# Rows of a shifted operand at other addresses: z at a step of 576 words, one word ahead of a multiple of 64 words

## The chip, the cores and the metric

The kernel runs on one core of one Trainium2 chip. The metric is the device time of one execution in microseconds (us). Runs of one kernel agree within about 0.2%.

## The reference

Two layers run one after the other on x (2048 rows of 512 numbers, float32). Each layer has two parts.

```
x = x + Re(DFT_seq(DFT_hidden(LN(x))))            # part A, matmuls with given cos/sin matrices
y = LN(x)                                         # part B takes y and returns
h = gelu(LN(y) @ w1)                              #   512 -> 512
hs = concat(h[:, 0:128] shifted by +1 row, h[:, 128:256] by -1,
            h[:, 256:384] by +2, h[:, 384:512] by -2) @ w2
x1 = y + hs
B(y) = x1 + gelu(LN(x1) @ w3) @ w4                #   512 -> 1376 -> 512
x = x + B(y)
```

## The kernel before

Every product is made of three fp32r matmuls: a number is split into a high part (its fp32r rounding, written by ACT) and a low part (the rest, written by DVE), and `mm3` (lines 277 to 280) adds high x high, high x low and low x high into one PSUM bank. The matrix that is multiplied is loaded as weights, 128 columns at a time (LDWEIGHTS), and the other operand streams past it, 512 float32 words a matmul. The two operands of a profile row are the ones it reads; for the matmuls on z the weights are w1 (`w`) and z (`zt`) streams.

Each layer first computes part A, in four chunks of 512 rows, and then calls `by_pairs`, which is part B. `by_pairs` begins with the same four chunks in order: `shifted(c)` is the product with w1 and the shift, `mixed(c)` the product with w2. After chunk 3 come two pairs of chunks of the MLP with w3 and w4, and while the second pair of layer 0 is worked on, part A of layer 1 is prepared.

**z.** The twice-normalized rows of a chunk, turned so that channels lie on the partitions, are called z: 4 channel tiles of 128, and for each a row of high parts and a row of low parts, 512 columns plus a halo of 2 columns at each end (`SW` = 516 words). There are two buffers: `zt[0]` for even chunks and `zt[1]` for odd ones (line 91); `ztf` are the same places read as plain float32. The shift of part B is done by reading: for the channel group g, `shifted` streams 512 words from the row's column 2 + `SHIFT[g]`, with `SHIFT` = (-1, 1, -2, 2), for each of the 4 channel tiles, so 12 matmuls a group. The groups run in the order -1, -2, +1, +2.

**How z is filled.** The normalized rows are turned by DVE, stored to DRAM (`turn_out`, line 600, four transfers on the SP queue) and fetched back as float32 into the places of the low parts (`turn_in`, line 605, one transfer of all four channel tiles). ACT then writes the high parts (`z_highs`, `high` at line 422) and DVE the low ones in place (`z_lows`, `low` at line 425), in two instructions each, two channel tiles at a time (`z_half`). The halo columns are zero at the ends of the sequence (`edges`), or copied from the chunk before by POOL (`left_halo`, line 626), or taken from the first two rows of the next chunk, which PE transposes (`right_halo`, lines 619 to 623). `turn_in` of chunk 1 is issued while chunk 0 is multiplied, and so on.

**Order.** The work beside the matmuls is laid into slots by hand: eight slots a chunk (four groups of `shifted`, four row tiles of `mixed`); `D(slot, ...)` runs ahead of the slot's own evacuation and `A(slot, ...)` after it. In each of them the instructions go to their engine's queue in the order written. SP issues all transfers in order, and the transfers signal their landing on eight semaphores that are used in turn.

**Places.** One arena of SBUF holds everything; tensors are placed by hand at word offsets from its start, which is byte 640 of each partition. `ZW` = 4128 words is the room of one z buffer; both stand at the arena's start. The weights w1 and w2 (`w12`, from word 8256), the streamed DFT blocks (`ring`) and the MLP's blocks all begin at multiples of 64 words. The four raw buffers (from `RAWS`, 1024 words each) receive DFT blocks and w1, w2 from DRAM in part A; in part B the same words are `rest[0]` to `rest[7]` (512 words each): `rest[0:4]` hold rows of odd chunks, `rest[4:8]` are used in the MLP pairs. Buffers that overlap are kept apart by waits that the framework puts in from the order of the program.

Of the kernel before, what the change touches and what calls it, by code (L numbers as in the profile page):

```python
# [8 lines left out]
F32 = mybir.dt.float32  # L9
F32R = mybir.dt.float32r  # L10
AF = mybir.ActivationFunctionType
ALU = mybir.AluOpType
# [7 lines left out]
CH = 512  # L20
NC = S // CH
TC = CH // P
KD = D // P
# [6 lines left out]
SHIFT = (-1, 1, -2, 2)  # L30
HALO = 2
SW = CH + 2 * HALO
RING = 4
RAW = 4
WARM = 12
# [7 lines left out]
def spectral_mlp_kernel(ctx: ExitStack, tc: tile.TileContext, x, ws, hs, w1, w2, w34, out):  # L43
    nc = tc.nc
# [23 lines left out]

    ZW = KD * 2 * SW
    AX, AY = 3 * 2 * DH, 4 * 2 * DH  # L70
# [5 lines left out]
    base = -(-nc.sbuf_base // 32) * 32  # L76
    EXT = RNG + RING * 4 * CH
    RAWS = EXT + 6 * D
# [3 lines left out]
    def at(name, word, *shape, dtype=F32R):  # L82
        return nc.alloc_sbuf_tensor_at(name, [P, *shape], dtype, offset=base + 4 * word).ap()

    def both(name, word, *shape):
        return at(name, word, *shape), at(name + "f", word, *shape, dtype=F32)
# [1 line left out]
    ay_at = (0, AY, H3, H3 + AY, EXT, 2 * AY, 3 * AY, 4 * AY)  # L88
    ay, ayf = zip(*(both(f"ay{k}", ay_at[k], 4, 2, DH) for k in range(NP)))
    ax, axf = zip(*(both(f"ax{k}", XS - 8 * D + k * AX, 3, 2, DH) for k in range(NP)))  # L90
    zt, ztf = zip(*(both(f"zt{i}", i * ZW, KD, 2, SW) for i in range(2)))
    w12 = [at(f"w12{i}", W12 + i * 4 * CH, 2, 2, CH) for i in range(4)]
    beside = at("beside", XS - 4 * D - 2 * HALO * KD * 2, 4, D, dtype=F32)
    xs = [at(f"xs{i}", XS + i * 2 * D, 2, D, dtype=F32) for i in range(NP)]
# [4 lines left out]
    rg = [[at(f"rg{i}{g}", RR + (4 * i + g) * 2 * CH, 2, CH) for g in range(KD)] for i in range(2)]  # L99
    ring, ringf = zip(*(both(f"ring{i}", RNG + i * 4 * CH, 2, 2, CH) for i in range(RING)))  # L100
    raw_at = [at(f"raw{i}", RAWS + i * 2 * CH, 2, CH, dtype=F32) for i in range(RAW)]
# [25 lines left out]
    def mm_bank():  # L127
        count["mm"] += 1
        return mm4[(count["mm"] - 1) % 4]
# [13 lines left out]
    def piece(src, a=0, b=2):  # L143
        pieces.append((src, a, b))
        return len(pieces) - 1
# [9 lines left out]
    for layer in range(LAYERS):  # L155
        for c in range(NC):
# [5 lines left out]
            for k in range(NP):  # L162
# [4 lines left out]
                p = piece(ws[c, k][:, 2:4])  # L167
# [42 lines left out]
    def stage_one():  # L210
# [4 lines left out]
        if dest is None:  # L215
            dest = ring[state["made"] % RING]
            sums[n] = ringf[state["made"] % RING][:, :, 1]
            state["made"] += 1
# [15 lines left out]
    def stage_two():  # L234
        n = state["two"]
        kind, ids, (a, b), _ = items[n]
        dest = slots[n]
        hi, lo = dest[:, a:b, 0], dest[:, a:b, 1]
        src = raws[ids[0]][:, a:b] if kind == "plain" else sums.pop(n)[:, a:b]
        for i in ((1, 0) if n == 1 else (slice(0, b - a),)):  # L240
            nc.vector.tensor_tensor(lo[:, i], src[:, i], hi[:, i].bitcast(F32), op=ALU.subtract)  # L241
        state["two"] += 1
        issue_dma()

    def room():
# [3 lines left out]
        if items[n][3] is not None:  # L249
            return True  # L250
        return state["made"] - state["done"] < RING

    def prefetch():
        n = state["one"]
        while room():
            stage_one()
            while state["two"] < state["one"] - 1:
                stage_two()
        while state["two"] < n:
            stage_two()  # L260
# [5 lines left out]
    def stream():  # L266
        i = state["use"]
        if i and items[i - 1][3] is None:
            state["done"] += 1
        state["use"] += 1  # L270
        prefetch()
        while state["two"] <= i:
            stage_two()
        return slots.pop(i)


    def mm3(o, lh, ll, rh, rl, first, last):
        nc.tensor.matmul(o, lh, rh, start=first, stop=False)  # L278
        nc.tensor.matmul(o, lh, rl, start=False, stop=False)  # L279
        nc.tensor.matmul(o, ll, rh, start=False, stop=last)  # L280
# [140 lines left out]
    def high(tf):  # L421
        nc.scalar.copy(tf[0][:, :, 0], tf[1][:, :, 1])

    def low(tf):
        nc.vector.tensor_tensor(tf[0][:, :, 1], tf[1][:, :, 1], tf[0][:, :, 0].bitcast(F32), op=ALU.subtract)
# [40 lines left out]
    def run_late(*names):  # L466
        for i in names:
            for f in late.pop(i, ()):
                f()
# [132 lines left out]
    def turn_in(dst, col):  # L602

        z = zd[count["turn"] % 2].rearrange("(d p) t -> p d t", p=P)
        nc.sync.dma_start(dst[:, :, 1, col : col + CH], z)

    def edges(c):

        if c == 0:
            nc.vector.memset(zt[0][:, :, :, :HALO].bitcast(F32), 0.0)  # L610
            left_halo(1)
        if c == NC - 1:
            nc.vector.memset(zt[c % 2][:, :, :, HALO + CH :].bitcast(F32), 0.0)

    def right_halo(c, u):

        ps = mm_bank()
        for d in range(KD):
            nc.tensor.transpose(ps[:, d * B : (d + 1) * B], u[:B, d * P : (d + 1) * P], ident[:B, :B])
        v = ps[:, : KD * B].rearrange("p (d t) -> p d t", d=KD)[:, :, :HALO]  # L620
        hi, lo = (zt[c % 2][:, :, i, HALO + CH :] for i in range(2))
        nc.scalar.copy(hi, v)
        nc.vector.tensor_tensor(lo, v, hi.bitcast(F32), op=ALU.subtract)

    def left_halo(c):
        nc.gpsimd.tensor_copy(zt[c % 2][:, :, :, :HALO], zt[(c - 1) % 2][:, :, :, CH : CH + HALO].bitcast(F32))

    def gelu(g, ps):
        order = "p (q b j) -> p b q j", "p (b q j) -> p b q j"
# [17 lines left out]
    def gelu_split(dst, ps, copy=nc.vector.tensor_copy):  # L647
        g = tmp_tile()
        gelu(g, ps)
        split(dst, g, copy)  # L650

    def shifted(c, w1p, hook=None, copy=nc.vector.tensor_copy, pre=None):

        for n, g in enumerate((0, 2, 1, 3)):
            ps = mm_bank()
            w = slice(HALO + SHIFT[g], HALO + SHIFT[g] + CH)
            for d in range(KD):
                s = w1p[d // 2][:, d % 2]
                z = zt[c % 2][:, d]
                v = slice(g * P, (g + 1) * P)  # L660
                mm3(ps, s[:, 0, v], s[:, 1, v], z[:, 0, w], z[:, 1, w], d == 0, d == KD - 1)
            if pre:
                pre(n)
            gelu_split(rg[c % 2][g], ps, copy)
            if hook:
                hook(n)
# [54 lines left out]
    def last_of(layer):  # L721
        return layer == LAYERS - 1

    def z_half(c, i):
        return [t[c % 2][:, 2 * i : 2 * i + 2, :, HALO : HALO + CH] for t in (zt, ztf)]

    def by_pairs(layer, zs, xin, dst):
        act = nc.scalar.copy
# [4 lines left out]
        turn_out(turned01)  # L733
        state["limit"] += 2
        w2p = [stream(), stream()]
        us = [[tmp[:, i] for i in range(4)], rest[0:4]]
        x1s, mrs, todo = {c: us[c % 2] for c in range(NC)}, {c: [] for c in range(NC)}, {}

# [49 lines left out]
            return lambda: [low((blk[b], blkf[b])) for b in names]  # L788

        def z_highs(c):  # L790
            return lambda: [high(z_half(c, i)) for i in range(2)]

        def z_lows(c):
            return lambda: [low(z_half(c, i)) for i in range(2)]

# [233 lines left out]
        for pair in range(n_pairs):  # L1031
# [11 lines left out]
            if pair == 0:  # L1043
                t = tmp[:, 0:4]
# [18 lines left out]
            for i, names in enumerate((("11", "21"), ("12", "22"))):  # L1063
                for d in range(KD):
                    b = blk[names[d // 2]]
                    v = slice(d * P, (d + 1) * P)
# [33 lines left out]
            for p in range(NF // 2):  # L1100
                prep = {} if kept else w_prep(p)
                u, v, x, y = sets[p % 2]
                w = w3b[(5 * pair + p) % 2]
# [89 lines left out]
            if last:  # L1193
                ss = [w4_use(), w4_use()]
                for q in range(TC):
                    v = slice(q * P, (q + 1) * P)
# [3 lines left out]
                    j = c2 * TC + q  # L1200
# [9 lines left out]
    for layer in range(LAYERS):  # L1210
# [4 lines left out]
        for c in range(NC):  # L1215
            if layer == 0 and c == 0:
# [58 lines left out]
                def hook(i):  # L1275
                    k, odd = divmod(i, 2)
                    state["limit"] = w_items[layer]
                    if not odd:
                        if k + 1 < NP:
                            xp_norm(k + 1, 3)  # L1280
                            xp_main(k + 1)
                        if not k:
                            xp_main_lows(1)
                    else:
                        if 0 < k < NP - 1:
                            xp_main_lows(k + 1)
                        if k + 2 < NP:
                            xp_stats(k + 2)
                        if k:
                            xp_sums(k - 1)  # L1290
                            xp_highs(k - 1, False)
                            xp_lows(k - 1, False)
# [62 lines left out]
        for i, (ri, dp) in enumerate(HORDER):  # L1355
            if i == 1:
                run_late("im1")
            if i == 3:
                state["limit"] += 2
            s = stream()  # L1360
            hid(ri, dp, s, acc4, 0, i == 0, i == 3)
            if i == 0:
                turn_in(ztf[0], HALO)
            if i < 2:
                j = (6, 8)[i]
                rows(xs[j // 2], x1d, j, 2, True)
            if i == 0:
                run_late("re1", "im1+")
            if i == 1:
                for half in range(2):  # L1370
                    high(z_half(0, half))
                run_late("re0+", "re0++")
                zs.update(norm_z((4, 5)))
            if i == 2:
                run_late("re0")
                for half in range(2):
                    low(z_half(0, half))
                zs.update(norm_z((6, 7)))
        by_pairs(layer, zs, xin, out if last_layer else x2d)

# [52 lines left out]
```

## Time and profile before

| what | value |
|---|---|
| median of 3 runs | 1445.81 us (1445.06 to 1447.05) |
| the profiled execution | 1445.1 us, span 1443.0 us, granted TensorE clock 1.000 |
| PE busy | 1434.9 us, 99% of the span, 6312 matmuls |
| DVE, ACT, POOL busy | 1127.5, 714.2, 82.2 us |
| DMA | 291.06 MB, mean 202 GB/s |
| chunks of `shifted` and `mixed`, layer 0 | about 410 to 500 us of the span |
| the same, layer 1 | about 1123 to 1213 us |

A row of instructions grouped by line reads: line, engine, operation, out<-in by the program's names, shape, count | busy us, mean ns of one | idle time of the engine before them and what ended it. A row in order of time reads: start us, length us, engine, line, operation, out<-in, and in brackets the idle time before it. The lengths of matmuls are longer than the distance between their starts, since they overlap. The chain of waits follows the work that ended last back from the end, at each step to what released it.

### The profile page before, as it was taken

The page shows a single profiled execution, that of the slowest core. Times are in us where ns is not written, and L with a number is a line of the kernel's source. Part 1 is how long each engine was busy: PE and PEld are TensorE (multiplying, and loading weights), DVE is VectorE, ACT ScalarE, POOL GpSimd, SP SyncE. Part 2 cuts the span into 40 slices and gives each one's busy share as a digit, 9 for nine tenths or more (in the row PEclk, how much of TensorE's full clock was granted, in tenths as well). Part 3 has the DMA queues.
Part 4 walks back from the last instruction along what each step waited for, and adds up shares of the span by engine and source line. Part 5 has one row for each costly group of instructions (what it writes and reads, how often), then busy time and mean ns, then how long its engine had stood idle before and what let it go on. Part 6 is the DMA issues. An engine that isn't in the chain of part 4 may idle for free.

```text
span 1443.0 us, 17233 instructions
## 1 busy us (share of the span) xinstructions
PE 1434.9 (99%) x6312; PEld 1180.7 (82%) x6312; DVE 1127.5 (78%) x1559; ACT 714.2 (49%) x954; POOL 82.2 (6%) x111
## 2 busy tenths in 40 slices
PE   9999999999999999999999999999999999999998
PEld 7888888888888787888888888888888888888887
DVE  7876997987979889656799979879898787656443
ACT  5563454455566755434555544544455574433231
POOL 2100000000001000000000000000000010000000
PEclk9999999999999999999999999999999999999999
DMA  7326655657655758954645556465766466579434
GB/s 251 128 88 206 202 188 198 198 181 258 205 173 136 265 206 289 363 196 164 216 158 195 175 197 211 161 227 167 228 224 233 132 175 262 182 244 338 155 130 161
DMA packets 116068, 291.06 MB, mean 202 GB/s; under 512 B 8592, under 2 KB 41360, under 8 KB 113424
## 3 DMA queue, kind: packets, MB, share of 16 engines
q1 hardware_dynamic: 115984, 289.97, 59.7%
q8 instruction: 49, 0.80, 0.2%
q14 instruction: 35, 0.29, 0.1%
HBM read 243.01 MB, written 46.92 MB: 201 GB/s over the span
## 4 chain that ended last, share of the span: by engine, by line
PE 88%; DVE 6%; ACT 2%; DMA 2%; issue 1%; SPq 0%; POOL 0%; DVEq 0%; ACTq 0%; POOLq 0%
PE psd L278 9%; PE psd L280 9%; PE psd L279 9%; PE psa L278 7%; PE psa L280 7%; PE psa L279 7%; PE psc L278 6%; PE psc L279 6%; PE psc L280 6%; PE psb L278 6%; PE psb L279 6%; PE psb L280 6%; DMA w4r<-w4d 1%; DVE st L292 1%; DMA zt1f<-zd 1%
## 5 line engine op out<-in xcount | busy, mean ns | idle before, releaser
L223 ACT CAST ring<-raw 128x1024 fp32r<-128x1024 f32 x127 | 133.1, 1053 | 99.8 <-PE psd L280 51.1
L241 DVE TENSOR_TENSOR ring<-raw,ring 128x1024 fp32r<-128x1024 f32 (+1 forms) x128 | 154.6, 1212 | 25.0 <-ACT ring L223 25.0
L278 PE MATMUL psd<-ring,rr 128*128 128x512 f32 x208 | 80.9, 389 | 0.0
L279 PE MATMUL psd<-ring,rr 128*128 128x512 f32 x208 | 80.9, 389 | 0.0
L280 PE MATMUL psd<-ring,rr 128*128 128x512 f32 x208 | 80.9, 389 | 0.0
L631 ACT ACTIVATE tmp<-rest 128x512 f32<-128x512 f32 x36 | 22.7, 632 | 94.8 <-DVE rest L464 94.5
L318 POOL TENSOR_TENSOR rs<-ve,mhalf 128x4 f32<-128x4 f32 x16 | 27.8, 1738 | 610.9 <-DVE nm L317 610.9
L230 ACT CAST ring<-ring0f 128x1024 fp32r<-128x1024 f32 x28 | 29.6, 1056 | 58.2 <-DVE ring0f L229 58.2
L634 DVE TENSOR_TENSOR h<-hc,h 128x512 fp32r<-128x512 f32 x41 | 27.9, 689 | 36.3 <-ACT h L637 34.6
L241 DVE TENSOR_TENSOR ring<-ring1f,ring 128x512 fp32r<-128x512 f32 (+1 forms) x56 | 53.3, 951 | 0.7 <-ACT ring L226 0.7
L297 POOL TENSOR_TENSOR rs<-ve,mhalf 128x2 f32<-128x2 f32 (+1 forms) x33 | 28.1, 853 | 417.2 <-DVE nb L296 417.2
L637 ACT CAST h<-hc 128x512 fp32r<-128x512 f32 x41 | 25.4, 621 | 51.2 <-PE psd L279 17.0
L279 PE MATMUL psb<-ring,ay 128*128 128x512 f32 x128 | 50.0, 391 | 0.0
L279 PE MATMUL psc<-ring,ay 128*128 128x512 f32 x128 | 49.9, 390 | 0.0
L280 PE MATMUL psb<-ring,ay 128*128 128x512 f32 x128 | 49.8, 389 | 0.0
L278 PE MATMUL psc<-ring,ay 128*128 128x512 f32 x128 | 49.8, 389 | 0.0
L280 PE MATMUL psc<-ring,ay 128*128 128x512 f32 x128 | 49.8, 389 | 0.0
L278 PE MATMUL psb<-ring,ay 128*128 128x512 f32 x128 | 49.8, 389 | 0.0
L280 PE MATMUL psa<-ring,ay 128*128 128x512 f32 x126 | 49.0, 389 | 0.0
L279 PE MATMUL psa<-ring,ay 128*128 128x512 f32 x126 | 49.0, 389 | 0.0
L278 PE MATMUL psd<-ring,ay 128*128 128x512 f32 x126 | 49.0, 389 | 0.0
L279 PE MATMUL psd<-ring,ay 128*128 128x512 f32 x126 | 49.0, 389 | 0.0
(444 smaller groups left out, 4417.3 us busy)
## 6 DMA issues: line engine op xcount, KB each, us to landing
raw<-in_ws SPq DMA_DIRECT2D x183, 512.0 KB, 4.9
w4r<-w4d SPq DMA_DIRECT2D x77, 512.0 KB, 4.1
raw<-in_hs SPq DMA_DIRECT2D x56, 512.0 KB, 3.6
w3b<-w3d SPq DMA_DIRECT2D x15, 1792.0 KB, 7.5
w3d<-w3b SPq DMA_DIRECT2D x5, 1792.0 KB, 6.3
x1d<-tmp SPq DMA_DIRECT2D x12, 512.0 KB, 6.2
xs<-x1d SPq DMA_DIRECT2D x12, 512.0 KB, 6.4
w4d<-w4r SPq DMA_DIRECT2D x11, 512.0 KB, 7.6
```

The source lines that it names most:

```text
L223: nc.scalar.copy(dest[:, a:b, 0], r[0][:, a:b])
L230: nc.scalar.copy(dest[:, :, 0], lo)
L241: nc.vector.tensor_tensor(lo[:, i], src[:, i], hi[:, i].bitcast(F32), op=ALU.subtract)
L278: nc.tensor.matmul(o, lh, rh, start=first, stop=False)
L279: nc.tensor.matmul(o, lh, rl, start=False, stop=False)
L280: nc.tensor.matmul(o, ll, rh, start=False, stop=last)
L292: nc.vector.bn_stats(st[:, i], s)
L297: nc.gpsimd.tensor_tensor(rs[:, :n], ve[:, :n], mhalf[:, 0, :n], op=ALU.pow)
L318: nc.gpsimd.tensor_tensor(rs, ve, mhalf[:, :, :2], op=ALU.pow)
L631: nc.scalar.activation(g_of, ps_of, AF.Gelu_apprx_tanh)
L634: nc.vector.tensor_tensor(dst[:, 1], g, dst[:, 0].bitcast(F32), op=ALU.subtract)
L637: copy(dst[:, 0], g)
```

## The change

Rows of z lie `ZP` = 576 words apart instead of 516. Each tensor of z begins 7 words ahead of its first row, so that the rows begin at word 63, 639, ... of the arena: one word ahead of a multiple of 64 words (256 bytes), counted from the arena's start. Four tiles of 2 x 576 words and a second such buffer don't fit in the room, so the odd chunks' buffer has three channel tiles there, and the fourth in the words of raw buffers 2 and 3 (`rest[4]` to `rest[6]`), which nothing else uses while z of an odd chunk lives. Each z is now a list of tensors (one for even chunks, two for odd), and everything that touches z goes through them: `turn_in`, `right_halo` and `left_halo` take one instruction for each tensor, `z_parts` gives pieces of two, one and one channel tiles for odd chunks. `left_halo(1)` moves from `edges(0)` to after the staging of w2 (in `by_pairs`, behind `w2p = [stream(), stream()]`).

```
+ZP = 9 * 64
...
-    zt, ztf = zip(*(both(f"zt{i}", i * ZW, KD, 2, SW) for i in range(2)))
+    zt, ztf = [], []
+    for i, places in enumerate((((56, 4),), ((56 + 8 * ZP, 3), (RAWS + 4 * CH + 56, 1)))):
+        ts = [both(f"zt{i}{j}", word, 7 + n * 2 * ZP) for j, (word, n) in enumerate(places)]
+        for z, k in ((zt, 0), (ztf, 1)):
+            z.append([t[k][:, 7:].rearrange("p (d r w) -> p d r w", r=2, w=ZP)[:, :, :, :SW] for t in ts])
...
     def turn_in(dst, col):
         z = zd[count["turn"] % 2].rearrange("(d p) t -> p d t", p=P)
-        nc.sync.dma_start(dst[:, :, 1, col : col + CH], z)
+        for d, t in z_rows(dst):
+            nc.sync.dma_start(t[:, :, 1, col : col + CH], z[:, d])
+
+    def z_rows(ts):
+        at = 0
+        for t in ts:
+            yield slice(at, at + t.shape[1]), t
+            at += t.shape[1]
+
+    def z_of(c, d):
+        return next(t[:, d - v.start] for v, t in z_rows(zt[c % 2]) if v.start <= d < v.stop)
 
     def edges(c):
         if c == 0:
-            nc.vector.memset(zt[0][:, :, :, :HALO].bitcast(F32), 0.0)
-            left_halo(1)
+            for t in zt[0]:
+                nc.vector.memset(t[:, :, :, :HALO].bitcast(F32), 0.0)
...
-        hi, lo = (zt[c % 2][:, :, i, HALO + CH :] for i in range(2))
-        nc.scalar.copy(hi, v)
-        nc.vector.tensor_tensor(lo, v, hi.bitcast(F32), op=ALU.subtract)
+        for d, t in z_rows(zt[c % 2]):
+            hi, lo = (t[:, :, i, HALO + CH :] for i in range(2))
+            nc.scalar.copy(hi, v[:, d])
+            nc.vector.tensor_tensor(lo, v[:, d], hi.bitcast(F32), op=ALU.subtract)
 
     def left_halo(c):
-        nc.gpsimd.tensor_copy(zt[c % 2][:, :, :, :HALO], zt[(c - 1) % 2][:, :, :, CH : CH + HALO].bitcast(F32))
+        for d, odd in z_rows(zt[1]):
+            even = zt[0][0][:, d]
+            to, of = (even, odd) if c % 2 == 0 else (odd, even)
+            nc.gpsimd.tensor_copy(to[:, :, :, :HALO], of[:, :, :, CH : CH + HALO].bitcast(F32))
...
-                z = zt[c % 2][:, d]
+                z = z_of(c, d)
...
-    def z_half(c, i):
-        return [t[c % 2][:, 2 * i : 2 * i + 2, :, HALO : HALO + CH] for t in (zt, ztf)]
+    def z_parts(c):
+        for t, tf in zip(zt[c % 2], ztf[c % 2]):
+            for d in range(0, t.shape[1], 2):
+                yield [z[:, d : min(d + 2, t.shape[1]), :, HALO : HALO + CH] for z in (t, tf)]
...
         w2p = [stream(), stream()]
+        left_halo(1)
```

More of the change, by code (lines that the diff above doesn't have):

```diff
@@ L604, in turn_in @@
         z = zd[count["turn"] % 2].rearrange("(d p) t -> p d t", p=P)
-        nc.sync.dma_start(dst[:, :, 1, col : col + CH], z)
+        for d, t in z_rows(dst):
[7 more added lines that the diff above has]
+        return next(t[:, d - v.start] for v, t in z_rows(zt[c % 2]) if v.start <= d < v.stop)
     def edges(c):
         if c == 0:
-            nc.vector.memset(zt[0][:, :, :, :HALO].bitcast(F32), 0.0)
-            left_halo(1)
+            for t in zt[0]:
+                nc.vector.memset(t[:, :, :, :HALO].bitcast(F32), 0.0)
         if c == NC - 1:
-            nc.vector.memset(zt[c % 2][:, :, :, HALO + CH :].bitcast(F32), 0.0)
+            for t in zt[c % 2]:
+                nc.vector.memset(t[:, :, :, HALO + CH :].bitcast(F32), 0.0)
     def right_halo(c, u):
@@ L790, in z_highs @@
         def z_highs(c):
-            return lambda: [high(z_half(c, i)) for i in range(2)]
+            return lambda: [high(z) for z in z_parts(c)]
         def z_lows(c):
-            return lambda: [low(z_half(c, i)) for i in range(2)]
+            return lambda: [low(z) for z in z_parts(c)]
         fs = [NF - 1] + list(range(NF - 1))
@@ L1369, in spectral_mlp_kernel @@
             if i == 1:
-                for half in range(2):
-                    high(z_half(0, half))
+                for z in z_parts(0):
+                    high(z)
                 run_late("re0+", "re0++")
@@ L1375, in spectral_mlp_kernel @@
                 run_late("re0")
-                for half in range(2):
-                    low(z_half(0, half))
+                for z in z_parts(0):
+                    low(z)
                 zs.update(norm_z((6, 7)))
```

## The prediction

> **What bounds the kernel now.** I read the page's shares first, then the PE instructions grouped by line with shapes apart, then single PE rows in order of time, and last the chain of waits where it leaves PE.
>
> ```profile
> span 1443.0 us, 17233 instructions
> PE 1434.9 (99%) x6312; PEld 1180.7 (82%) x6312; DVE 1127.5 (78%) x1559; ACT 714.2 (49%) x954; POOL 82.2 (6%) x111
> ...
> PE 88%; DVE 6%; ACT 2%; DMA 2%; issue 1%; SPq 0%; POOL 0%; DVEq 0%; ACTq 0%; POOLq 0%
> ```
>
> PE is never free for long, and 88% of the chain is matmuls. So the time is the number of matmuls by the distance between their starts, plus a few short stalls. The change removes no matmul; it can only alter that distance, or a stall.
>
> ```profile
> L278 PE MATMUL psd<-ring,rr 128*128 128x512 f32 x208 | 80.9, 389 | 0.0
> ...
> L278 PE MATMUL psd<-zt,w 128*128 128x512 f32 x68 | 27.0, 398 | 0.0
> ...
> L278 PE MATMUL psa<-zt,w 128*128 128x512 f32 x60 | 24.1, 402 | 0.0
> ```
>
> Of matmuls of one shape, those that stream z (zt) are the long ones: 398 and 402 ns against 389. There are 384 of them: 2 layers x 4 chunks x 4 shifts x 4 channel tiles x 3 products. The durations overlap, so I price by starts. First and last rows of groups of 12 z matmuls (one chunk, one shift), and of 36 that stream w2:
>
> ```profile
> 410.28 0.40 PE L278 MATMUL psd<-zt,w 128*128 128x512 f32 x1
> ...
> 412.88 0.40 PE L280 MATMUL psd<-zt,w 128*128 128x512 f32 x1
> ...
> 416.46 0.39 PE L278 MATMUL psa<-zt,w 128*128 128x512 f32 x1
> ...
> 418.98 0.40 PE L280 MATMUL psa<-zt,w 128*128 128x512 f32 x1
> 419.21 0.40 PE L278 MATMUL psd<-zt,w 128*128 128x512 f32 x1
> ...
> 421.75 0.39 PE L280 MATMUL psd<-zt,w 128*128 128x512 f32 x1
> ...
> 424.75 0.39 PE L278 MATMUL psa<-w,rg 128*128 128x512 f32 x1
> ...
> 432.69 0.39 PE L280 MATMUL psd<-w,rg 128*128 128x512 f32 x1
> ...
> 441.85 0.40 PE L278 MATMUL psd<-zt,w 128*128 128x512 f32 x1
> ...
> 444.42 0.39 PE L280 MATMUL psd<-zt,w 128*128 128x512 f32 x1
> ...
> 481.00 0.39 PE L278 MATMUL psd<-zt,w 128*128 128x512 f32 x1
> ...
> 483.54 0.40 PE L280 MATMUL psd<-zt,w 128*128 128x512 f32 x1
> ```
>
> The ordinary distance is (432.69-424.75)/35 = 226.9 ns. Now the addresses, in words from the start of the arena. Before, rows of z begin at multiples of 516 and 4128, all multiples of 4, and a matmul starts 2 + shift words further on: one word past a multiple of 4 for shift -1, three past it for +1, on it for -2 and +2. Shift -1 (chunk 0): 2.60/11 = 236.4 ns. Shift +1: 2.52/11 = 229.1. Shift +2: 230.9 in chunk 0 and 2.57/11 = 233.6 in chunk 1. Shift -2 (chunk 3): 230.9. For starts on a multiple of 4 I use 232.0. The order of the four does not follow the order of time, so it goes with the address. The whole excess is 96 x (9.5 + 2.2 + 5.1 + 5.1) ns = 2.1 us, 0.15% of the span: the most that placement by itself can bring.
>
> **The change part by part.**
>
> (a) New starts. Rows lie 63 words past a multiple of 64, so the starts are 0 (shift -1), 2 (+1), 63 (-2) and 3 (+2) past it. Shift -1 now starts on a multiple of 64, as every ring, weight and block operand does (their offsets, 8256, 16448 and so on, are multiples of 64): between 226.9 and 232.0; I take 226.9, as the address is of the ordinary kind. Gain 96 x 9.5 = 0.91 us. Shifts -2 and +2 are now three past a multiple of 4, the class of the 229.1 row: 192 x 2.9 = 0.56 us. Shift +1 is two past it, a class that no row shows: between 226.9 and 236.4, and as it lies between the one-past and three-past classes I take the middle, 231.7, a loss of 96 x 2.6 = 0.25 us. Sum 1.22 us: 0.61 a layer, 0.31 for two chunks. Bounds: 2.1 us; and with shift -1 at 232.0, +1 at 236.4 and the others unchanged, 0.42 - 0.70 = a loss of 0.3 us.
>
> [...]
>
> (b) Smaller pieces for the odd chunks. A high or low of z was two instructions of 1024 elements; for odd chunks it is one of 1024 and two of 512.
>
> ```profile
> L637 ACT CAST h<-hc 128x512 fp32r<-128x512 f32 x41 | 25.4, 621 | 51.2 <-PE psd L279 17.0
> ...
> L634 DVE TENSOR_TENSOR h<-hc,h 128x512 fp32r<-128x512 f32 x41 | 27.9, 689 | 36.3 <-ACT h L637 34.6
> ```
>
> ```profile
> L422 ACT CAST zt<-zt1f x8: 1038/1055/1058, 424.8 to 1185.7; 128x1024 fp32r<-128x1024 f32 x8
> L425 DVE TENSOR_TENSOR zt<-zt1f,zt x8: 1226/1227/1228, 427.0 to 1188.1; 128x1024 fp32r<-128x1024 f32 x8
> L626 POOL CAST zt<-zt x6: 198/200/1229, 407.3 to 1165.5; 128x16 fp32r<-128x16 f32 x6
> ...
> L622 ACT CAST zt<-psa x3: 158/158/158, 437.1 to 1172.9; 128x8 fp32r<-128x8 f32 x3
> ```
>
> ACT: 2 x 621 - 1055 = 0.19 us more four times; DVE: 2 x 689 - 1227 = 0.15 us more four times. The right halo of chunk 1 has one more ACT piece of 0.16 us and one more DVE piece; each left halo one more POOL piece of 0.20 us. POOL is busy 6%, ACT 49%: I price these at nothing except where (d) shows DVE to be late; without that cover they would add about 0.5 us a layer.
>
> (c) The left halo of chunk 1 moves behind both transposes and the staging of w2, because its last tile's place is raw buffer 2 and 3, which w2's lows still read.
>
> ```profile
> 407.26 1.21 POOL L626 CAST zt<-zt 128x16 fp32r<-128x16 f32 x1 [45.18 <-ACT w L223]
> ...
> 411.89 2.31 DVE L241 TENSOR_TENSOR w<-raw,w 128x1024 fp32r<-128x1024 f32 x2
> ...
> 418.73 0.38 SPq L605 DMA_DIRECT2D zt1f<-zd  x1
> ```
>
> It can run from 414.20 instead of 407.26, 1.2 us or less a piece. Nothing else stands behind it on POOL then. SP's transfer, which fills the same buffers, issues at 418.73, and the first matmul that reads the halo follows the row at 432.69. It passes the four stores of turned z on SP, which do not touch it. Cost nothing, with 2 us to spare.
>
> (d) The transfer of z in two, for odd chunks: three tiles, then one; same bytes, one issue (0.38 us) more. This matters in one place, layer 0, chunk 3, where the chain leaves PE at the end of chunk 1 and comes back 46 us later:
>
> ```profile
> 444.85 0.61 ACT extra L631
> ...
> 490.57 0.61 DVE rg L634
> 491.18 0.04 issue
> 491.23 0.50 PE psa L280
> ```
>
> ```profile
> 463.81 0.89 SPq L605 DMA_DIRECT2D zt1f<-zd  x1
> ...
> 470.73 0.80 ACT L326 ACTIVATE tmp<-xs,nb,rs 128x512 f32<-128x512 f32 x1
> 472.36 2.14 ACT L422 CAST zt<-zt1f 128x1024 fp32r<-128x1024 f32 x2 [0.84 <-DMA zt1f<-zd]
> ...
> 474.59 2.49 DVE L425 TENSOR_TENSOR zt<-zt1f,zt 128x1024 fp32r<-128x1024 f32 x2 [2.45 <-ACT zt L422]
> ...
> 490.23 0.39 PE L279 MATMUL psa<-w,rg 128*128 128x512 f32 x1
> 491.23 0.50 PE L280 MATMUL psa<-w,rg 128*128 128x512 f32 x1 [0.61 <-DVE rg L634]
> ```
>
> PE loses 1.00 - 0.23 = 0.77 us there. The first low of z waited for both highs (it starts 0.09 us after 472.36 + 2.14), although it reads only the first's tiles. With the last tile a buffer of its own, it should wait for the first two pieces only: 472.36 + 1.06 + 0.62 + 0.11 = 474.15, and lows of 1.23 + 0.69 + 0.69 end at 476.8 against 477.08: 0.3 us earlier. The first transfer, three quarters of the bytes, can also land earlier; ACT has been free since 471.53, so that is worth 0 to 0.83 us; it shares the queue with stores, and I take a quarter, 0.2. Relief 0.5 us (bounds -0.2, if DVE waits for all three highs, and 1.1).
>
> **The sum.** In layer 0 the chain goes with PE to 444.85 (0.31 us gained by two chunks), then with DMA, ACT and DVE (0.5 us). PE itself arrives 0.61 us earlier at 490, so 0.57 us of stall remain and what is gained is 0.8 us, not 0.61 + 0.77. Layer 1 shows no such stall and keeps its 0.61 us. Total 1.4 us. The profiled execution took 1445.1 us (span 1443.0), 0.7 below the median of the runs, 1445.81; taken from the median, 1444.4 us.
>
> **The rivals.** 1, all of it: shift +1 and the others also come down to 226.9 and the stall goes: 2.1 + 0.8 = 2.9 us, 1442.9. For it: every other operand runs at 226.9. Against: no start three past a multiple of 4 does so in the groups shown.
>
> [...]
>
> 3, slower: the transfers go round eight semaphores, so four more transfers shift which earlier landing each later issue waits for. The place is the second half of the first MLP pair.
>
> ```profile
> SPq L818 <- DMA w4d<-w4r: 7.1, 2, 6.2
> ```
>
> ```profile
> 594.80 13.80 DMA w4r<-w4d
> 608.75 0.47 PE psc L278
> ```
>
> There a load of w4 takes 13.8 us and PE starts as it lands; SP has waited up to 6.2 us for a landing before such a load. If one such wait moves ahead of this load, PE waits as long: with 6.2 us, 1444.4 + 6.2 = 1450.6. It decides from about 1.4 us on (no gain left), and passes 0.2% above from 4.3 us on. Against it: two extra transfers a layer, each in a stretch where SP waits for data rather than for a queue.
>
> **How the numbers follow.** My forecast 0.66, rival 1 0.12, rival 2 0.13, rival 3 0.09. A measurement of this kernel tells about 0.2%, 2.9 us, from no change. Nearly all of the forecast and rival 2, half of rival 1 (it lies on the bound) and half of rival 3 are within: faster 0.08, same 0.87, slower 0.05. Range: down past half of rival 1, 1442.6; up past rival 2 and the loss bound of (a), 1446.3.
>
> **What would show it.** In the profile after, groups of 12: shift -1 at 227 ns, -2 and +2 at 229, +1 near 232; the L278 zt groups' mean near 393. In layer 0, chunk 3: the first low of z 1.8 us after the first high starts, and a shorter wait at the L280 matmul. The left halo of chunk 1 near 414. Wrong would be: shift +1 above 236, shift -1 above 232, a new releaser in PE's waits, or w4r landing later.

## The result and the profile after

The changed kernel takes 1503.71 us (median of 4, 1503.04 to 1504.46) against 1445.43: a ratio of 1.0402, with a 95% interval of 1.0390 to 1.0415. It is 58 us slower, where 1444.4 was forecast. The page of the profile after, its shares, the granted clock by slices and the chain by engine:

```profile
span 1502.0 us, 17276 instructions
...
PE 1454.2 (97%) x6312; PEld 1190.5 (79%) x6312; DVE 1129.3 (75%) x1567; ACT 714.7 (48%) x960; POOL 80.3 (5%) x117
...
PEclk9999999999998999999999999999999899999999
...
PE 80%; DVE 8%; DMA 5%; ACT 5%; issue 2%; SPq 0%; POOL 0%; DVEq 0%; POOLq 0%; ACTq 0%
```

DVE and ACT work as long as before. PE has lost share of the chain, DMA has gained it, and two of the slices show less than full clock; before, none did. PE's waits after, longest first (engine, line, what was waited for: us in total, times, longest):

```profile
PE psa L283 <- DMA zt10f<-zd: 11.4, 2, 5.8
PE psd L283 <- DMA zt10f<-zd: 9.3, 2, 4.7
PE psd L283 <- DMA zt00f<-zd: 5.7, 1, 5.7
PE psa L283 <- DMA zt00f<-zd: 5.4, 1, 5.4
PE psa L284 <- ACT zt L640: 2.5, 4, 0.6
PE psa L283 <- POOL zt L647: 2.2, 1, 2.2
PE psd L283 <- POOL zt L647: 2.2, 1, 2.2
...
PE psd L284 <- ACT zt L640: 1.2, 2, 0.6
```

None of these eight stood in the profile before. They sum to 31.8 us for transfers, 4.4 for POOL, 3.7 for ACT. Which transfer is the point. The first one, in order of time (chunk 0, last matmul of shift -2 and first of +1):

```profile
418.31 0.39 PE L285 MATMUL psa<-zt,w 128*128 128x512 f32 x1
424.30 0.80 PE L283 MATMUL psa<-zt,w 128*128 128x512 f32 x1 [5.60 <-DMA zt10f<-zd]
424.89 0.63 PE L284 MATMUL psa<-zt,w 128*128 128x512 f32 x1
425.32 0.63 PE L285 MATMUL psa<-zt,w 128*128 128x512 f32 x1
```

Chunk 0 streams the even buffer, zt00, but it waited for the transfer that fills the odd one, zt10, which only chunk 1 reads. The same happens in chunk 1 (for zt00) and chunk 2 (for zt10), in both layers; chunk 3, with no transfer of z behind it, is spared. In the program the transfer for the next chunk stands between the groups with shift -2 and +1 of each of these chunks, and it is at +1 that PE waits. Behind each such wait matmuls start 0.43 us apart instead of 0.23. By the distances between starts, the 384 z matmuls took 144.2 us against 90.5, 53.7 of the 59.0 us by which the span grew; the two waits on POOL, 4.4 us, stand ahead of a group's first matmul and are not among them.

The stretches of half clock in this trace are, up to the last matmul, 3.41 or 6.83 us long and begin on one grid (in layer 0 at 423.35, 454.07, 477.96 and 491.61, which is 9, 7 and 4 times 3.41 us apart). Windows of 3.41 us on that grid show when the clock goes down (us, PE busy and number of matmuls, granted clock, DMA share, GB/s):

```profile
416.52:419.93 3.41, 2.18 (x9) 1.00 0.67 162
419.93:423.35 3.42, 0.00 (x0) 1.00 0.60 203
423.35:426.76 3.41, 2.46 (x6) 0.50 1.03 392
426.76:430.17 3.41, 3.41 (x10) 0.50 0.47 173
430.17:433.58 3.41, 3.41 (x17) 1.00 0.00 0
...
474.55:477.96 3.41, 1.19 (x6) 1.00 0.52 114
477.96:481.37 3.41, 3.41 (x10) 0.50 0.94 217
481.37:484.79 3.42, 2.79 (x13) 1.00 0.94 240
484.79:488.20 3.41, 1.73 (x8) 1.00 0.26 61
488.20:491.61 3.41, 0.42 (x2) 1.00 0.90 331
491.61:495.03 3.42, 3.42 (x10) 0.50 1.05 401
```

Here a window in which PE was busy for 1.19 us or less was followed by one at half clock; after one with 1.73 us the clock stayed; half clock ended one full window of work later. In layer 1 windows with 1.20 and 1.34 us were followed by half clock too. So a wait of 5.6 us cost two windows at half clock as well.

My theory was then: the two z buffers share words. The even one is declared from word 56 with 7 + 4608 words, so it ends at 4671, and the odd one begins at 4664. No row of z lies in the shared 7 words, but the framework orders accesses by what is declared, and if two tensors overlap it lets each access of one wait for each earlier write of the other. The rival: the new addresses, or the third place, slow PE or the transfers by themselves.

### The profile page after: what moved, and what is told of

Read it like the earlier page. It is cut to its first block, busy times and chain, and to the rows that moved or that the text cites. A ratio compares the mean times of both kernels' runs of the same rounds, so it can differ in the third digit from the quotient of the medians.

```text
span 1502.0 us, 17276 instructions
## 1 busy us (share of the span) xinstructions
PE 1454.2 (97%) x6312; PEld 1190.5 (79%) x6312; DVE 1129.3 (75%) x1567; ACT 714.7 (48%) x960; POOL 80.3 (5%) x117
## 4 chain that ended last, share of the span: by engine, by line
PE 80%; DVE 8%; DMA 5%; ACT 5%; issue 2%; SPq 0%; POOL 0%; DVEq 0%; POOLq 0%; ACTq 0%
PE psd L283 9%; PE psd L284 8%; PE psd L285 8%; PE psa L283 7%; PE psa L284 7%; PE psa L285 7%; PE psc L283 6%; PE psc L284 6%; PE psc L285 6%; PE psb L284 6%; PE psb L283 6%; PE psb L285 6%; DMA zt00f<-zd 2%; DMA zt10f<-zd 1%; ACT tmp L331 1%
## 5 line engine op out<-in xcount | busy, mean ns | idle before, releaser
L283 PE MATMUL psd<-ring,rr 128*128 128x512 f32 x208 | 80.9, 389 | 0.0
L655 DVE TENSOR_TENSOR rg<-extra,rg 128x512 fp32r<-128x512 f32 x32 | 22.1, 692 | 77.9 <-ACT rg L658 77.9
L283 PE MATMUL psc<-ring,ay 128*128 128x512 f32 x128 | 49.8, 389 | 0.0
L283 PE MATMUL psb<-ring,ay 128*128 128x512 f32 x128 | 49.8, 389 | 0.0
L283 PE MATMUL psa<-ring,ay 128*128 128x512 f32 x126 | 49.0, 389 | 0.0
L283 PE MATMUL psd<-ring,ay 128*128 128x512 f32 x126 | 49.0, 389 | 0.0
```

Source lines behind the costliest of these rows:

```text
L655: nc.vector.tensor_tensor(dst[:, 1], g, dst[:, 0].bitcast(F32), op=ALU.subtract)
```

## The experiments

**Buffers apart, same addresses** (e1_apart). Rows of 576 words are declared, and z is taken from column 7; every row of z stays on the word that the change gave it.

```
-        ts = [both(f"zt{i}{j}", word, 7 + n * 2 * ZP) for j, (word, n) in enumerate(places)]
+        ts = [both(f"zt{i}{j}", word, n, 2, ZP) for j, (word, n) in enumerate(places)]
...
-            z.append([t[k][:, 7:].rearrange("p (d r w) -> p d r w", r=2, w=ZP)[:, :, :, :SW] for t in ts])
+            z.append([t[k][:, :, :, 7 : 7 + SW] for t in ts])
```

> Same word addresses of every row of z as in the changed kernel, but each tensor of z is declared as rows of 576 words and its rows are taken from column 7 on, so that the even chunks' tensor ends at word 4664, where the odd chunks' first tensor begins (in the changed kernel they share words 4664 to 4670). False-wait theory: the matmuls on z no longer wait for the other buffer's transfer, no matmul runs at 427 ns, and what is left is the gain of the new addresses, 384 x (232.5 - 229.3) = 1.2 us, and up to 0.5 us of relief in chunk 3 of layer 0: 1443 to 1445 us. Address theory (the rows' new places or the third place in the raw buffers slow PE or its transfers): the time stays at 1503.

Measured: 1443.69 us (median of 11) against 1445.36, ratio 0.9988 (0.9979 to 0.9997). The address theory is out: with the same addresses the 58 us are gone, and the kernel is 1.7 us faster than before, the lowest median of all. Its shares, and its PE waits from the second on (the first is the start of the kernel):

```profile
PE 1433.4 (99%) x6312; PEld 1180.4 (82%) x6312; DVE 1127.5 (78%) x1567; ACT 714.9 (50%) x960; POOL 85.4 (6%) x117
```

```profile
PE psc L283 <- DVE rest L469: 1.0, 1, 1.0
PE psc L283 <- DMA w4r<-w4d: 0.9, 1, 0.9
PE psc L284 <- DVE ring L246: 0.7, 1, 0.7
```

No wait of PE on z is left.

**The shared words alone** (e3_share). As e1_apart, with the odd buffer declared 8 words earlier and its rows taken from column 15, so that all rows stay where they were.

```
-    ... (((56, 4),), ((56 + 8 * ZP, 3), (RAWS + 4 * CH + 56, 1)))
+    ... (((56, 4),), ((48 + 8 * ZP, 3), (RAWS + 4 * CH + 56, 1)))
...
-            z.append([t[k][:, :, :, 7 : 7 + SW] for t in ts])
+            z.append([t[k][:, :, :, skip : skip + SW] for t, skip in zip(ts, (7 + 8 * i, 7))])
```

> The same as the run before in every address, but the odd chunks' first tensor is declared from word 4656 on (rows from column 15), so that it shares 8 words with the even chunks' tensor; no row of z lies in them. False-wait theory: the waits of the changed kernel come back, three a layer of 5 to 6 us on the other buffer's transfer, with slow matmuls behind them: 1495 to 1505 us. If it was the flat declaration with rearranged views that made the waits, not the shared words: 1443 to 1445.

Measured: 1501.71 us, one run. The first wait again, in order of time:

```profile
423.17 0.77 PE L283 MATMUL psa<-zt,w 128*128 128x512 f32 x1 [6.80 <-DMA zt10f<-zd]
```

The two programs read and write the same words; only the declared bounds differ, by 8 words that hold nothing. That is 1501.7 - 1443.7 = 58.0 us.

**The same at the old addresses** (b1_share_old).

```
-    zt, ztf = zip(*(both(f"zt{i}", i * ZW, KD, 2, SW) for i in range(2)))
+    zt, ztf = zip(*(both(f"zt{i}", i * ZW, KD + 1 - i, 2, SW) for i in range(2)))
+    zt, ztf = ([t[:, :KD] for t in ts] for ts in (zt, ztf))
```

> The kernel before, with one thing changed: the even chunks' tensor of z is declared one channel tile longer, so that it runs over the first tile of the odd chunks' tensor; all addresses, transfers and instructions stay. False-wait theory: PE waits three times a layer for the other buffer's transfer, at the start of the group with shift +1, and runs at about 427 ns for some us behind each: 1490 to 1505 us. Address theory: nothing changes, 1445.

Measured: 1509.01 us, one run, 4 above the expected span of times; the kernel before, made 64 us slower by a declaration.

```profile
425.33 0.76 PE L279 MATMUL psa<-zt,w 128*128 128x512 f32 x1 [7.87 <-DMA zt1f<-zd]
```

The wait is longer than the changed kernel's 5.60 us. Here z comes as one transfer of all four tiles, while in the changed kernel the fourth tile lies apart and PE waits for three; that this is the difference was not tried by itself.

**PE kept at work** (f1_filled). The changed kernel, with its waits, and 26 more matmuls where PE would stand.

```
+            if n == 2 and c < NC - 1:
+                for i in range(26):
+                    nc.tensor.matmul(ps, w1p[0][:, 0, 0, :P], w1p[0][:, 0, 0], start=True, stop=True)
```

> The changed kernel with 26 extra matmuls on w1 alone (5.9 us, overwritten by the group that follows) in front of the group with shift +1 of chunks 0 to 2, so that PE works while it would wait; the waits themselves stay. If the matmuls at 427 ns come from PE having stood still, they vanish behind these six waits: 64 x 0.2 us and the first slow ones, some 14 us, less 1 to 3 us by which the filling is longer than the shortest waits: 1489 to 1493 us. If they come from how z is read or from transfers that land, they stay: 1503 or more.

Measured: 1493.98 us, one run, 1 us above what I expected. 156 more matmuls (35 us of PE's time) make the kernel 9.7 us faster than the change (1503.71).

```profile
418.51 6.07 PE L680 MATMUL psa<-w 128*128 128x512 f32 x26
```

The mean granted clock is 0.999 against 0.986, and of the 64 z matmuls that started 400 to 440 ns apart, 61 of them at half clock, 11 are left. Seven stand in a row at half clock in layer 1 (1209.7 to 1212.7), behind the 2.2 us wait on POOL, which was not filled; the other four are single ones at full clock, 400 to 402 ns. So the low clock comes from PE's standing still. I had put the gain at 11 to 15 us; the filling is longer than the waits it covers, all of which vanish from the list.

**Apart, but declared flat** (e2_flat_apart).

```
-    ... ((56 + 8 * ZP, 3), (RAWS + 4 * CH + 56, 1))
+    ... ((56 + 8 * ZP + 64, 3), (RAWS + 4 * CH + 56, 1))
```

> The changed kernel with one number changed: the odd chunks' first tensor stands 64 words further on (from word 4728), so that it shares no word with the even chunks' tensor; the flat declaration with rearranged views stays, and so do the row step and the place of the rows within 64 words. Shared-words theory: all waits on the other buffer's transfer go, and the 0.6 us waits on the right halo's ACT copy too: 1443 to 1446 us. If the flat declaration makes waits of its own (on the ACT copies of the right halo, 3.7 us in the changed kernel), those stay: about 1448 to 1450.

Measured: 1450.13 us, one run. All waits for transfers of z are gone; two rows of waits on z are left, six waits in all:

```profile
PE psa L284 <- ACT zt L640: 2.5, 4, 0.6
...
PE psd L284 <- ACT zt L640: 1.2, 2, 0.6
```

So the flat declaration does make waits of its own, as the second of the two expectations had it, and 6.4 us against e1_apart. My reading, which is argued and not shown: the right halo is written in two columns of each row; declared flat, with rearranged views, this write stretches over everything between the first row and the last, and the next group's second matmul (row of low parts) waits for it; its first matmul, whose words end below the halo's first column, doesn't. It fits which matmul waits; a flat declaration at the old addresses was not run.

**The pieces alone** (s1_pieces). Old row step and addresses, the odd chunks' fourth tile in the raw buffers' words, two transfers and the smaller pieces.

```
-ZP = 9 * 64
+ZP = SW
...
+    for i, places in enumerate((((0, 4),), ((ZW, 3), (RAWS + 4 * CH, 1)))):
+        ts = [both(f"zt{i}{j}", word, n, 2, ZP) for j, (word, n) in enumerate(places)]
+            z.append([t[k] for t in ts])
```

> The pieces alone: rows 516 words apart at the old addresses for the even chunks and the odd chunks' first three tiles (declared apart, no word shared), the odd chunks' fourth tile in the raw buffers' words, with the two transfers, the smaller high and low pieces and the later left halo of the change. If the gain of the run with tensors apart (1443.7 against 1445.4) is the new start addresses in PE's reading, this one gains at most the 0.9 us stall in chunk 3 of layer 0 and may lose it again behind: 1444.5 to 1445.8, with the z matmuls at 232 ns as before. If the gain is the pieces', it stands at 1443.7.

Measured: 1445.35 us (median of 11) against 1445.73, ratio 0.9996 (0.9987 to 1.0005). The pieces by themselves show no change. In its profile the 0.77 us stall of chunk 3, layer 0, is gone, and PE's wait for w4 has grown from 0.2 to 1.2 us.

**Rows at another place** (e4_row60).

```
-            z.append([t[k][:, :, :, 7 : 7 + SW] for t in ts])
+            z.append([t[k][:, :, :, 4 : 4 + SW] for t in ts])
```

> As the run with tensors apart, but rows from column 4: they begin 60 words past a multiple of 64, so that the starts are 61 (shift -1), 63 (+1), 60 (-2) and 0 (+2). If the price of a start goes by its distance to a multiple of 64 words, as the new rows suggest (0: 227.0 ns, 63: 227.7, 3: 228.9, 2: 234.4), with 61 and 60 at the 229 to 230 that single old rows there show: mean 228.5 against 229.5 ns, 0.4 us less than that run. If it goes by the residue by 4 (one past: 236, on it: 232): mean 231, 0.6 us more.

Measured: 1444.64 us (median of 11), ratio 0.9995 (0.9986 to 1.0004): not to be told from e1_apart's. The distances from each of z's matmuls to the next start, leaving out those over 300 ns beside a transpose, tell more: start 61: 233.0 ns, 63: 228.4, 60: 234.3, 0: 227.5, mean 230.8. Neither expectation held: the mean is that of the residues (231), but 60 and 0 are both multiples of 4 and differ by 6.8 ns.

## Why the prediction was wrong

**The step that failed is (c), and with it the list of rivals.** There I asked which reads and writes the moved left halo and the new place must wait for, by the words that hold data. I never laid the declared bounds of the new tensors side by side: 56 + 7 + 4608 = 4671 against 4664. The sum has no term for it, and (c) ends with "Cost nothing"; the runs give the shared words 58.0 us (e3_share against e1_apart). The flat declaration has no term either: it cost 6.4 us by itself (e2_flat_apart against e1_apart), and 2.0 us where words were shared as well (1503.71 against 1501.71, one run), so the two costs do not add up. "What would show it" did name a new releaser in PE's waits, and that is where it showed.

The clue stood in (d). There the first low of z had waited for both highs, though it reads only one's tiles, and I took it that waits go by declared buffer, and used this for a gain of 0.3 us. The same rule, turned on the new declarations, would have raised the question whether buffers that share a word wait for each other.

**Rival 3** ended on the right side by the wrong mechanism. It looked for the loss in a w4 load in the first MLP pair. The load did move a little (a wait of 0.9 us in e1_apart, 0.2 before), less than the 6.2 us that rival 3 priced, and the 58 us are not there.

**The price of a wait** was missed too: nothing in the sum counted the clock. Of the 59.0 us of span, the eight rows of waits make 39.9; of the rest, 12.7 us are the 64 z matmuls that started 400 to 440 ns apart instead of 227; the last 6.4 us I did not split. In the profile after, a window with PE busy for 35% (1.19 of 3.41 us) was followed by half clock, and one with 51% (1.73 us) was not.

**What was right, by the run without the shared words:**

- (a), the new starts. Predicted 226.9 (shift -1), 229.1 (-2), 229.1 (+2) and 231.7 ns (+1); measured in e1_apart 227.0, 227.7, 228.9 and 234.4. The gain over all z matmuls is 90.46 - 89.34 = 1.1 us, predicted 1.2. The class that no row showed, two past a multiple, was the worst of the four and lay 2.7 ns above the middle of its bounds. That the total came out is luck in part: shift +1 lost 0.26 us more than forecast, -2 gained 0.13 us more. The classes by 4 that stand behind it do not hold: 63 and 3 are both three past a multiple of 4 and differ by 1.2 ns, and 60 and 0, both on one, by 6.8 (e4_row60). The lengths of the L283 matmuls on z, forecast near 393 ns, came down less, from 398 and 402 to 396 and 399. First and last rows of the four groups (-1, -2, +1, +2) of chunk 3, layer 0, in e1_apart:

```profile
478.08 0.39 PE L283 MATMUL psa<-zt,w 128*128 128x512 f32 x1
...
480.57 0.39 PE L285 MATMUL psa<-zt,w 128*128 128x512 f32 x1
480.80 0.39 PE L283 MATMUL psd<-zt,w 128*128 128x512 f32 x1
...
483.30 0.39 PE L285 MATMUL psd<-zt,w 128*128 128x512 f32 x1
483.52 0.40 PE L283 MATMUL psd<-zt,w 128*128 128x512 f32 x1
...
486.10 0.40 PE L285 MATMUL psd<-zt,w 128*128 128x512 f32 x1
486.34 0.39 PE L283 MATMUL psa<-zt,w 128*128 128x512 f32 x1
...
488.85 0.39 PE L285 MATMUL psa<-zt,w 128*128 128x512 f32 x1
```

- (d), the pieces. In e1_apart, chunk 3 of layer 0, the highs begin as ACT comes free, and the first low 1.79 us after the first high, predicted 1.8:

```profile
471.37 1.70 ACT L427 CAST zt<-zt10f 128x1024 fp32r<-128x1024 f32 x2
```

```profile
473.16 1.96 DVE L430 TENSOR_TENSOR zt<-zt10f,zt 128x1024 fp32r<-128x1024 f32 x2 [1.08 <-issue]
```

The low began 1.4 us earlier (473.16 against 474.59). The forecast has 0.6 for this start beside PE's own gain (474.59 - 474.15, and 0.2 for the transfer): it took a quarter of the 0.83 us that an earlier landing could bring, and the highs waited for no landing at all. The stall at 490 vanished. What it gave, the wait for w4 took back behind it, as s1_pieces shows by itself.
- The total without the shared words and the flat declaration, 1443.69, lies inside the range given, 0.7 us below the forecast of 1444.4. Of its 1.7 us the new starts explain 1.1; the rest is within the interval (0.4 to 3.0 us).
- Rival 1 is out, with shift +1 at 234.4 ns, and rival 2 (given 0.13: the new starts bring nothing) too: no run shows its loss, and in e1_apart the starts differ in price, 227.0 to 234.4 ns, and the new ones gain 1.1 us.

## What to carry to other kernels

When tensors are placed by hand, write down each one's first and last declared word, padding too, and compare neighbours: where a framework orders work by declarations, as here, words that two tensors share without using them can still make waits. When a change moves buffers, look in the waits for a releaser that the waiting instruction has no use for; the name of the tile in the row is enough to see it. Here a wait on PE cost more than its length once it left most of a 3.41 us window empty (1.19 us of PE in it, and 3.41 us at half clock behind), so price such a wait with the matmuls at half clock that follow.

## What the runs showed of the hardware

Matmuls that stream the same 512 words start 227.0 to 236.3 ns apart by where the words begin. In words past a multiple of 64, from e1_apart and e4_row60: 0: 227.0 and 227.5, 63: 227.7 and 228.4, 3: 228.9 (e1_apart), 61: 233.0, 60: 234.3 (e4_row60), 2: 234.4 (e1_apart); 236.3 is shift -1 in the kernel before. I know no rule that gives this order. Part of each figure is the start of a group: in e4_row60 the last 8 distances of groups at 63 (chunks 0 to 2) and at 0 are 226.6 to 226.8 ns, and in e1_apart, chunk 3, with no transpose ahead, 63 has 227.0. So these two starts run close to the 226.9 of the matmuls on w2, and 61, 60, 3 and 2 do not.

In the changed kernel the clock fell to half after a single wait of 2.2 us that lay within one window (474.55 to 477.96, above); in f1_filled, layer 0, the same wait lay across two windows and the clock stayed at full, as it did after the 1.2 us stall at 551.9 in the kernel before. Over all runs, coming from full clock, the busiest window that was followed by half clock had 1.45 us of PE (b1_share_old, 476.16 to 479.57), and the emptiest that was not, amid the matmuls, had 1.73 us (above).
